# Rows of w2 in runs of four, with a different split of its last 96 rows and a different place of TensorE's loop in its code

## The chip, the cores and the metric

The kernel runs on one core of a Trainium2 chip. The metric is the device time of one execution in microseconds (us), given as the median of several runs. Profiles come from one further execution each.

## The reference

One decoding step of a transformer layer for one token of width D = 512: attention over a cache of 32 heads with 32,768 keys of width 128 each, then a dense block with a mish activation of width F = 1376. All tensors are bf16.

```python
q = layernorm(x) @ wq                                   # (512) @ (512, 32*128)
scores = einsum("bhqd,bhkd->bhqk", q, k_cache) * 128**-0.5
o = einsum("bhqk,bhkd->bhqd", softmax(scores), v_cache)
h = x + o.reshape(1, 1, 4096) @ wo                      # (4096, 512)

t = layernorm(h) @ w1 + b1                              # (512, 1376)
act = t * tanh(softplus(t))
out = h + act @ w2                                      # (1376, 512)
```

The two caches are 32 x 8 MB each. With wq and wo (4 MB each) and w1 and w2 (1.4 MB each) the kernel reads 548 MB.

## The kernel before

**Data.** `ring` holds six slots of 32 KB per partition. Keys of a head take two slots, alternating between two homes; values take the next two. A head's 32,768 rows lie so that partition p holds the 256 rows from 256p on, 64 KB in one run. At the end, the slots of the keys are used again: one for wo, one (`WL`) for wo's last 128 rows, w1 (`w1_v`) and w2 (`w2_v`).

**The queue.** SP issues all loads, in the order of the list `order`: wq, k0, then k(h+1) and v(h) in turn, wo, the last v, `WL`, four quarters of w1, the parts of w2. A load waits until TensorE has finished with what its slot held (`freed_by`, `done_with`). The first and last heads' loads are cut into pieces with semaphores of their own.

**The loop.** TensorE and VectorE run the heads in a loop. In `_pe_rounds` TensorE's code is laid out as blocks `top`, `head`, `skip`, `mid`, `tail`, `turn`, `rest`, `over`. `head` transposes the 256 key tiles of a head (L685; VectorE copies them back, L691) and multiplies them by the query (L661). `rest` finishes the softmax of the head before and multiplies its 256 value tiles by the probabilities (L712). `turn` runs once, after the first `head`; `mid` and `tail` run after the last one. `t.addr_align(256, offset=100, max_nops=0)` puts the beginning of `top` at slot 100 of a block of 256 instructions.

**The dense block.** A unit of the hidden layer is one of F's 1376 columns of w1 and rows of w2. In `mid`, b1 is transposed into `b1c` (L786, L789), and the output projection of 31 heads runs (L798). In `tail` follow the last head's projection, the second layernorm, and then three steps:

- the hidden layer (L834): for each quarter `kc` of w1 and each column j of `hid_ps`, one matmul with one output column. There are FJ + 1 = 11 columns, ten of 128 units and one of 96;
- mish on [128, 11] (L841 to L849), giving `actT`;
- the output layer (L854): for each column j, four matmuls, one for each 128 columns of the output. They lie in four strips of the array.

Units are given to columns in pairs: w2's rows 2p and 2p + 1 of a group of 256 lie in partition p, so that a DMA moves runs of two rows (2 KB). Its last 96 rows are one row per partition. `W2_J = [0, 4, 8, FJ]` are the columns at which the four DMAs of w2 begin; the matmuls of L854 wait for each DMA's semaphore at its first column. The same pairs are read from w1 by a step of two elements (`w1_pairs`).

Of the kernel before, what the change touches and what calls it, by code (L numbers as in the profile page):

```python
# [6 lines left out]
BF16 = mybir.dt.bfloat16  # L7
F32 = mybir.dt.float32
I32 = mybir.dt.int32
# [13 lines left out]
class _Sched:  # L23
# [146 lines left out]
    def _pe_rounds(self, end, head, turn, rest, mid, tail):  # L170
        from concourse.ordered_engine_set import OrderedEngineSet
        nc, e, t = self.nc, LOOPED[PE], self.engines[PE]
        on = OrderedEngineSet([e])
        names = [f"rounds_{x}_{nc.next_id()}" for x in ("top", "head", "skip", "mid", "tail", "turn", "rest", "over", "done")]
        top, n_head, n_skip, n_mid, n_tail, n_turn, n_rest, n_over, done = names
        regs = nc.alloc_registers("round", engines=on)
        nc.regs_mov(regs, 0)
        t.addr_align(256, offset=100, max_nops=0)
        nc.br(top, engines=on)
        self.reg = regs[e]  # L180
        with nc.body(top, valid_engines=on):
# [126 lines left out]
def build_kernel(nc, A_x, A_k_cache, A_v_cache, A_wq, A_wo, B_w1, B_b1, B_w2, out):  # L308
# [22 lines left out]
    FJ = F // 128  # L331
    FLAST = F - FJ * 128
    W1 = KC * F
    assert HALVES == 2 and KC == 4 and H <= 32 and FLAST > 0 and FJ % 2 == 0
    assert KC * HD == SLOT and H * D == SLOT
    W2 = W1 + (FJ + 1) * D
    assert W2 + D <= SLOT
    WB = Dh // 32

# [37 lines left out]
    perm = sb([128, 128], BF16, "perm")  # L377
    oL = sb([128, 1], BF16, "oL")
    xr = sb([1, D], BF16, "xr")
    b1r = sb([FJ // 2 + 1, 256], BF16, "b1r")  # L380
# [4 lines left out]
    hsb = sb([128, 7, FJ + 1], F32, "hsb")  # L385
    b1c = sb([128, FJ + 1], F32, "b1c")
    actT = sb([128, FJ + 1], BF16, "actT")
    outr = perm

    S_ps = ps([128, 512], "sps")  # L390
# [7 lines left out]
    C_REG = hlp[:, 129:130]  # L398
    Q_REG = hlp[:, 160:160 + H]
    L_REG = hlp[:, 200:202]  # L400
    hid_ps = S_ps[:, 0:FJ + 1]
    X_REG = hlp[:, 204:204 + 2 * KC]
    B1_REG = T_f[3][:, 0:FJ + 1]
    B1_PAIRS = T_f[3][:, 0:FJ].rearrange("p (i s) -> p s i", s=2)
    y2_ps = T_f[0][:, 0:128]
    OX_PS = T_f[2][:, 0:32]

# [105 lines left out]
    w2_v = w12[:, W1:W2].rearrange("p (j n) -> p j n", j=FJ + 1)  # L513
    wol_v = w12[:, W2:W2 + D]

    def done_with(kind, h, r0, r1):
# [18 lines left out]
    def program(S):  # L535
# [13 lines left out]
        for what in order:  # L549
# [4 lines left out]
            flat = ring[:, slot, :]  # L554
            if what[0] == "wq":
                S.wait(SP, ["b1z"])
                start(b1r[0:FJ // 2, :], B_b1[0:FJ * 128].rearrange("(i p) -> i p", i=FJ // 2), s_b1)
                start(b1r[FJ // 2:FJ // 2 + 1, 0:FLAST], B_b1[FJ * 128:F].rearrange("(o p) -> o p", o=1), s_b1)
            elif what[0] == "wo":
                start(flat, A_wo.rearrange("(p j) n -> p (j n)", j=32), ready[slot])  # L560
            elif what == WL:
# [1 line left out]
            elif what[0] == "w1":  # L563
                k = what[1]
                start(w1_v[:, k, :], B_w1[k * 128:(k + 1) * 128, :], w1_sems[k])
            elif what[0] == "w2":
                n = what[1]
                if n + 1 < len(W2_J):
                    j0, j1 = W2_J[n], W2_J[n + 1]
                    start(w2_v[:, j0:j1, :].rearrange("p (i s) n -> p i (s n)", s=2),  # L570
                          B_w2[j0 * 128:j1 * 128, :].rearrange("(i p s) n -> p i (s n)", p=128, s=2), w2_sems[n])
                else:
                    start(w2_v[0:FLAST, FJ, :], B_w2[FJ * 128:F, :], w2_sems[n])
            else:
# [12 lines left out]
                for r, n in uncut(what) if kind == "v" else later_k(h):  # L587
                    S.dma(SP, lambda r=r, n=n: sp.sem_inc(cut_sems[kind][r], 16 * n))
# [192 lines left out]
                       name=("y" if c == KC - 1 else None), waits=([f"oev{H - 1}", ready_wait(WL)] if c == 0 else ()))  # L781

        def mid():
            n_b1 = FJ // 2 + 1
            for s in range(2):
                S.step(PE, lambda s=s: t_.matmul(B1_PAIRS[:, s, :], b1r[:, :].rearrange("i (q s) -> i s q", s=2)[:, s, :],  # L786
                                                 identb[0:n_b1, 0:FJ // 2], start=True, stop=True),
                       waits=([(s_b1, 32)] if s == 0 else ()))
            S.step(PE, lambda: t_.matmul(B1_REG[:, FJ:FJ + 1], b1r[:, 0:128], identb[0:n_b1, FJ // 2:n_b1], start=True, stop=True),  # L789
                   name="b1t")  # L790
# [16 lines left out]
        def tail():  # L807
# [17 lines left out]
            S.step(ACT, lambda: a.activation(lnv, nvar, ACTF.Ln, bias=epsc[:, 0:1], scale=-1.0), name="lnln1", waits=["lnvar1", "epsc"])  # L825
            S.step(ACT, lambda: a.activation(rstd, lnv, ACTF.Exp, scale=-0.5), name="lnr1", waits=["lnln1"])
            for kc in range(KC):
                for j in range(FJ + 1):
                    W = 128 if j < FJ else FLAST
                    cols = w1_pairs[:, kc, j // 2, j % 2, :] if j < FJ else w1_v[:, kc, j * 128:F]  # L830
                    last = j == FJ and kc == KC - 1
                    waits = [(w1_sems[kc], 16)] if j == 0 else []
                    waits += ["xc1", f"exp{H - 1}"] if j == 0 and kc == 0 else []
                    S.step(PE, lambda W=W, j=j, kc=kc, last=last, cols=cols: t_.matmul(  # L834
# [12 lines left out]
            S.step(DVE, lambda: v.tensor_scalar_add(den, u, 2.0), name="den", waits=["u"])  # L847
            S.step(DVE, lambda: v.reciprocal(rden, den), name="rden", waits=["den"])
            S.step(DVE, lambda: v.tensor_tensor(actT[:, :], hu, rden, ALU.mult), name="act", waits=["rden", "hu"])  # L849
            for j in range(FJ + 1):  # L850
                W = 128 if j < FJ else FLAST
                for c in range(KC):
                    last = j == FJ and c == KC - 1
                    S.step(PE, lambda W=W, j=j, c=c: t_.matmul(  # L854
                        y2_ps[32 * c:32 * c + 1, :], actT[0:W, j:j + 1], w2_v[0:W, j, c * 128:(c + 1) * 128],
                        start=False, stop=(j == FJ), skip_group_check=True),
                        name=("y2" if last else None),
                        waits=((["act"] if j == 0 else []) + [(w2_sems[W2_J.index(j)], 16)] if c == 0 and j in W2_J else ()))
            S.step(DVE, lambda: v.tensor_copy(outr[:, :], y2_ps), name="fin", waits=["y2"])  # L859
# [49 lines left out]
```

## Time and profile before

| | |
|---|---|
| median of 3 runs | 1275.71 us (1275.57 to 1275.84) |
| the profiled execution, as timed | 1275.48 us |
| its span in the profile | 1273.6 us |
| TensorE busy, matmuls | 1016.5 us (80%) |
| VectorE busy | 715.8 us (56%) |
| bytes moved | 548.35 MB, mean 431 GB/s |
| granted TensorE clock, mean | 0.77 |

The profile counts time from the first instruction. TensorE's matmuls (PE) and weight loads (PEld) stand apart. A row of a timeline begins with start and duration; "x16" counts the instructions that it merges, and the brackets tell the idle time ahead of it and what ended it. SPq is SP's issuing of DMAs. In the chain of waits, "issue" is time in which an engine waited for nothing that the profile shows.

### The profile page before, as it was taken

The numbers are of one execution on the slowest core, as the hardware profiler recorded it, in microseconds if no ns is written. First come the engines' busy times: TensorE is split into PE (matmuls) and PEld (weight loads), VectorE is DVE, ScalarE is ACT, GpSimd is POOL, SyncE is SP. The second block draws the span as 40 slices with busy tenths as digits, with TensorE's granted clock in tenths as the row PEclk, the third lists the DMA queues.
The fourth block names the chain that finished last, engine by engine and source line by source line (L and its number), as shares of the span: only waits on it lengthen the run. The fifth ranks groups of instructions, "written<-read, shape, count | busy, mean of one in ns | idle before, by whom it ended". The sixth has DMA issues, their size and how long they took to land.

```text
span 1273.6 us, 54445 instructions
## 1 busy us (share of the span) xinstructions
PE 1016.5 (80%) x25046; PEld 988.9 (78%) x25046; DVE 715.8 (56%) x1252; ACT 20.6 (2%) x71; POOL 0.9 (0%) x8
## 2 busy tenths in 40 slices
PE   4689877779777789777788777797777897777995
PEld 4689877779777789777788777797777887777994
DVE  2566664456654466644466644566544666445661
ACT  0000000000000000000000000000000000000000
POOL 0000000000000000000000000000000000000000
PEclk9888876778877688867788776787777887677885
DMA  9999999999999999999999999999999999999998
GB/s 403 445 417 437 432 438 434 440 428 428 432 438 430 445 428 428 430 440 428 445 430 428 430 438 430 440 434 428 428 438 432 434 440 428 428 436 434 426 435 353
DMA packets 12350, 548.35 MB, mean 431 GB/s; under 512 B 1360, under 2 KB 1590, under 8 KB 2998
## 3 DMA queue, kind: packets, MB, share of 16 engines
q1 hardware_dynamic: 12340, 548.22, 99.7%
q8 instruction: 8, 0.13, 0.0%
q10 hardware_dynamic: 2, 0.00, 0.0%
HBM read 548.21 MB, written 0.00 MB: 430 GB/s over the span
## 4 chain that ended last, share of the span: by engine, by line
DMA 54%; DVE 23%; PE 18%; issue 2%; SPq 2%; POOL 0%; POOLq 0%
DMA ring<-in_A_k_cache_dram 51%; DVE ering L691 23%; PE ops L712 9%; PE tps L685 6%; DMA ring<-in_A_v_cache_dram 2%; SPq L545 2%; PE sps L661 1%; DMA ring<-in_B_w_dram 1%; PE hlp L736 1%; PE hlp L731 1%; PE hlp L746 0%; PE tps L854 0%; DVE pmax L725 0%; DVE perm L859 0%; DVE gmax L733 0%
## 5 line engine op out<-in xcount | busy, mean ns | idle before, releaser
L685 PE MATMUL tps<-identb,ring 128*128 128x128 bf16 x8192 | 668.3, 232 | 209.4 <-DMA ring<-in_A_k_cache_dram 204.9
L691 DVE COPY ering<-tps 128x1024 bf16<-128x1024 bf16 x1024 | 669.4, 692 | 259.7 <-PE tps L685 258.5
L685 PEld LDWEIGHTS tps<-identb,ring 128*128 x8192 | 522.2, 104 | 212.2 <-issue 212.2
L661 PE MATMUL sps<-qcur,ering 128*128 128x1 bf16 x8192 | 343.7, 164 | 7.7 <-DVE ering L691 6.7
L661 PEld LDWEIGHTS sps<-qcur,ering 128*128 128x128 bf16 x8192 | 309.2, 97 | 10.7 <-DVE ering L691 9.4
L712 PEld LDWEIGHTS ops<-pbuf,ring 128*128 128x128 bf16 x8192 | 226.3, 103 | 24.4 <-issue 15.1
L712 PE MATMUL ops<-pbuf,ring 128*128 128x1 bf16 x8192 | 231.3, 165 | 10.8 <-DMA ring<-in_A_v_cache_dram 8.3
L720 DVE TENSOR_TENSOR oT<-ops,rtotc 128x1 f32 x31 | 5.0, 162 | 109.8 <-PE ops L712 109.8
L733 DVE TENSOR_REDUCE gmax<-hlp 1x1 f32<-1x128 f32 x32 | 8.9, 278 | 67.5 <-PE hlp L731 67.5
L738 DVE TENSOR_SCALAR nbias<-hlp 128x1 f32<-128x1 f32 x32 | 5.1, 158 | 63.4 <-PE hlp L736 63.4
L741 ACT ACTIVATE pbuf<-sps,nbias 128x256 bf16<-128x256 f32 x32 | 15.2, 474 | 1219.9 <-PE ops L712 1166.7
L731 PE MATMUL hlp<-ident,pmax 128*1 128x128 f32 x64 | 17.9, 379 | 5.2 <-issue 5.2
L725 DVE TENSOR_REDUCE pmax<-sps 128x1 f32<-128x256 f32 x32 | 13.6, 425 | 14.3 <-PE sps L661 14.3
L736 PE MATMUL hlp<-gmax,onesmat 1*128 1x1 f32 x64 | 18.5, 356 | 0.4 <-DVE gmax L733 0.4
L736 PEld LDWEIGHTS hlp<-gmax,onesmat 1*128 1x128 f32 x64 | 15.8, 304 | 1.3 <-DVE gmax L733 0.9
L746 PE MATMUL hlp<-esum,onesmat 128*128 128x1 f32 x64 | 12.1, 258 | 4.8 <-issue 1.0
L746 PEld LDWEIGHTS hlp<-esum,onesmat 128*128 128x128 f32 x64 | 9.5, 188 | 7.4 <-issue 7.4
L640 PE MATMUL hlp<-xnT,ring 128*128 128x1 bf16 x128 | 3.6, 165 | 9.2 <-DMA ring<-in_A_wq_dram 9.2
L640 PEld LDWEIGHTS hlp<-xnT,ring 128*128 128x128 bf16 x128 | 3.5, 104 | 9.3 <-issue 9.3
L720 DVE TENSOR_TENSOR oL<-ops,rtotc 128x1 bf16<-128x1 f32 x1 | 0.2, 161 | 14.3 <-PE ops L712 14.3
L731 PEld LDWEIGHTS hlp<-ident,pmax 128*1 128x1 f32 x64 | 2.8, 81 | 5.8 <-issue 5.3
L748 DVE RECIPROCAL rtotc<-hlp 128x1 f32<-128x1 f32 x32 | 5.4, 168 | 2.7 <-PE hlp L746 1.4
(77 smaller groups left out, 40.1 us busy)
## 6 DMA issues: line engine op xcount, KB each, us to landing
ring<-in_A_k_cache_dram SPq DMA_DIRECT2D x3, 4096.0 KB, 40.2
ring<-in_A_v_cache_dram SPq DMA_DIRECT2D x3, 4096.0 KB, 15.3
ring<-in_A_k_cache_dram SPq DMA_DIRECT2D x3, 2048.0 KB, 30.5
ring<-in_A_k_cache_dram SPq DMA_DIRECT2D x1, 6144.0 KB, 44.6
ring<-in_A_wq_dram SPq DMA_DIRECT2D x1, 4096.0 KB, 12.2
ring<-in_A_wo_dram SPq DMA_DIRECT2D x1, 4096.0 KB, 35.6
ring<-in_A_v_cache_dram SPq DMA_DIRECT2D x1, 2048.0 KB, 16.1
ring<-in_B_w_dram SPq DMA_DIRECT2D x4, 344.0 KB, 20.7
```

Source lines behind the costliest of these rows:

```text
L545: S.dma(SP, lambda: sp.dma_start(dst, src).then_inc(s, 16))
L640: S.step(PE, lambda h=h, kc=kc: t_.matmul(Q_REG[:, h:h + 1], wq_v[:, kc, h * Dh:(h + 1) * Dh], xnT[:, 0, kc:kc + 1], start=(kc == 0), stop ...
L661: S.step(PE, lambda r=r: t_.matmul(S_ps[:, col0 + r:col0 + r + 1], ering[:, bg % NE, r, :], qcur[:, :], start=True, stop=True), name=(name ...
L685: S.step(PE, lambda r=r, at=at: t_.matmul(tb[:, r * 128:(r + 1) * 128], key_tile(S, at), identb[:, :], is_transpose=True, start=True, stop ...
L691: S.step(DVE, lambda: v.tensor_copy(ering[:, bg % NE, :, :].rearrange("p r d -> p (r d)"), tb[:, :]), name=f"ev{bg}", waits=[f"trb{bg}"], ...
L712: S.step(PE, lambda r=r: t_.matmul(o_ps[:, 0:1], vt[:, r, :], pbuf[:, r:r + 1], start=(r == 0), stop=(r == SCOLS - 1)), name=(names or Non ...
L725: S.step(DVE, lambda: v.tensor_reduce(pmax[:, :], S_ps[:, 0:SCOLS], AXX, ALU.max), name=f"pmax{h}", waits=[f"qkh{h}"], kind="pmax")
L731: S.step(PE, lambda: t_.matmul(A_REG, pmax[:, :], ident[:, :], start=True, stop=True), name=f"A{h}", waits=[f"pmax{h}", "ident", f"rcp{h - ...
L733: S.step(DVE, lambda: v.tensor_reduce(gmax[:, :], A_REG, AXX, ALU.max), name=f"gmax{h}", waits=[f"A{h}"], kind="gmax")
L736: S.step(PE, lambda: t_.matmul(B_REG, onesm[0:1, :], gmax[:, :], start=True, stop=True), name=f"B{h}", waits=[f"gmax{h}", "consts0"] + ([] ...
L741: S.step(ACT, lambda: a.activation(pbuf[:, :], S_ps[:, 0:SCOLS], ACTF.Exp, bias=nb[:, :], scale=SC, accum_out=esum[:, :]), name=f"exp{h}", ...
L746: S.step(PE, lambda: t_.matmul(C_REG, onesm[:, :], esum[:, :], start=True, stop=True), name=f"C{h}", waits=[f"exp{h}"], kind="C")
```

## The change

Units are given to columns in fours instead of pairs. Rows 0 to 1023 of w2 go in two DMAs of 128 partitions by four rows (4 KB runs) to columns 0 to 3 and 4 to 7, rows 1024 to 1279 as before in pairs to columns 8 and 9. [...] So there are five DMAs of w2 instead of four, and FC = 15 columns instead of 11 in the hidden layer, in mish and in the output layer. w1 is read by the steps that belong to this (`units_of`), and b1 is loaded as three rows of 512 and transposed in 11 matmuls instead of 3. `identi` now shares the memory of `ering`. The loop of TensorE begins at slot 30 of a block instead of slot 100.

```diff
-        t.addr_align(256, offset=100, max_nops=0)
+        t.addr_align(256, offset=30, max_nops=0)
...
+    FC = FJ + 5
+    W2 = W1 + FC * D
...
-    identi = sb([128, 128], I32, "identi")
+    identi = ering[:, 1, 0:2, :].rearrange("p r d -> p (r d)").bitcast(I32)
...
-    W2_J = [0, 4, 8, FJ]
+    W2_G = [(0, 0, 4, 128), (4, 512, 4, 128), (8, 1024, 2, 128), (10, 1280, 4, 20), (14, 1360, 1, F - 1360)]
+    W2_J = [g[0] for g in W2_G]
+    W2_M = [next(m for j0, _, n, m in W2_G if j0 <= j < j0 + n) for j in range(FC)]
...
-    w1_pairs = w1_v[:, :, 0:FJ * 128].rearrange("p k (i q s) -> p k i s q", q=128, s=2)
+    def units_of(rows, j):
+        j0, u0, n, m = next(g for g in W2_G if g[0] <= j < g[0] + g[2])
+        return rows[:, u0:u0 + n * m].rearrange("p (q s) -> p s q", s=n)[:, j - j0, :]
...
             elif what[0] == "w2":
                 n = what[1]
-                if n + 1 < len(W2_J):
-                    j0, j1 = W2_J[n], W2_J[n + 1]
-                    start(w2_v[:, j0:j1, :].rearrange("p (i s) n -> p i (s n)", s=2),
-                          B_w2[j0 * 128:j1 * 128, :].rearrange("(i p s) n -> p i (s n)", p=128, s=2), w2_sems[n])
-                else:
-                    start(w2_v[0:FLAST, FJ, :], B_w2[FJ * 128:F, :], w2_sems[n])
+                j0, u0, c, m = W2_G[n]
+                src = B_w2[u0:u0 + c * m, :].rearrange("(p s) n -> p (s n)", s=c)
+                if m == 20:
+                    src = src.rearrange("(a p) n -> a p n", a=5)
+                start(w2_v[0:m, j0:j0 + c, :].rearrange("p s n -> p (s n)"), src, w2_sems[n])
...
             for kc in range(KC):
-                for j in range(FJ + 1):
-                    W = 128 if j < FJ else FLAST
-                    cols = w1_pairs[:, kc, j // 2, j % 2, :] if j < FJ else w1_v[:, kc, j * 128:F]
+                for j in range(FC):
+                    W = W2_M[j]
+                    cols = units_of(w1_v[:, kc, :], j)
...
-            for j in range(FJ + 1):
-                W = 128 if j < FJ else FLAST
+            for j in range(FC):
+                W = W2_M[j]
                 for c in range(KC):
```

More of the change, by code (lines that the diff above doesn't have):

```diff
@@ L333, in build_kernel @@
     W1 = KC * F
-    assert HALVES == 2 and KC == 4 and H <= 32 and FLAST > 0 and FJ % 2 == 0
+    assert HALVES == 2 and KC == 4 and H <= 32 and FLAST > 0 and FJ == 10
     assert KC * HD == SLOT and H * D == SLOT
-    W2 = W1 + (FJ + 1) * D
+    FC = FJ + 5
+    W2 = W1 + FC * D
     assert W2 + D <= SLOT
@@ L384, in build_kernel @@
     xnT = sb([128, 2, KC], BF16, "xnT")
-    hsb = sb([128, 7, FJ + 1], F32, "hsb")
-    b1c = sb([128, FJ + 1], F32, "b1c")
-    actT = sb([128, FJ + 1], BF16, "actT")
+    hsb = sb([128, 7, FC], F32, "hsb")
+    b1c = sb([128, FC], F32, "b1c")
+    actT = sb([128, FC], BF16, "actT")
     outr = perm
@@ L400, in build_kernel @@
     L_REG = hlp[:, 200:202]
-    hid_ps = S_ps[:, 0:FJ + 1]
+    hid_ps = S_ps[:, 0:FC]
     X_REG = hlp[:, 204:204 + 2 * KC]
-    B1_REG = T_f[3][:, 0:FJ + 1]
-    B1_PAIRS = T_f[3][:, 0:FJ].rearrange("p (i s) -> p s i", s=2)
+    B1_REG = T_f[3][:, 0:FC]
     y2_ps = T_f[0][:, 0:128]
@@ L511, in build_kernel, with __getitem__ @@
     w1_v = w12[:, 0:W1].rearrange("p (k n) -> p k n", k=KC)
-    w1_pairs = w1_v[:, :, 0:FJ * 128].rearrange("p k (i q s) -> p k i s q", q=128, s=2)
-    w2_v = w12[:, W1:W2].rearrange("p (j n) -> p j n", j=FJ + 1)
+    class b1_last:
+        def __getitem__(self, at):
+            return b1r[:, at[1].start - 1024:at[1].stop - 1024]
+    def units_of(rows, j):
+        j0, u0, n, m = next(g for g in W2_G if g[0] <= j < g[0] + g[2])
+        return rows[:, u0:u0 + n * m].rearrange("p (q s) -> p s q", s=n)[:, j - j0, :]
+    w2_v = w12[:, W1:W2].rearrange("p (j n) -> p j n", j=FC)
     wol_v = w12[:, W2:W2 + D]
@@ L556, in program @@
                 S.wait(SP, ["b1z"])
-                start(b1r[0:FJ // 2, :], B_b1[0:FJ * 128].rearrange("(i p) -> i p", i=FJ // 2), s_b1)
-                start(b1r[FJ // 2:FJ // 2 + 1, 0:FLAST], B_b1[FJ * 128:F].rearrange("(o p) -> o p", o=1), s_b1)
+                start(b1r[0:2, :], B_b1[0:1024].rearrange("(i p) -> i p", i=2), s_b1)
+                start(b1r[2:3, 0:F - 1024], B_b1[1024:F].rearrange("(o p) -> o p", o=1), s_b1)
             elif what[0] == "wo":
@@ L783, in mid @@
         def mid():
[L784 to L790, printed above, removed]
+            for n in range(4):
+                S.step(PE, lambda n=n: t_.matmul(B1_REG[:, 0:8].rearrange("p (i s) -> p s i", s=4)[:, n, :],
+                                                 b1r[:, :].rearrange("i (q s) -> i s q", s=4)[:, n, :],
+                                                 identb[0:3, 0:2], start=True, stop=True),
+                       waits=([(s_b1, 32)] if n == 0 else ()))
+            for j in range(8, FC):
+                S.step(PE, lambda j=j: t_.matmul(B1_REG[0:W2_M[j], j:j + 1], units_of(b1_last(), j), identb[0:3, 2:3], start=True, stop=True),
+                       name=("b1t" if j == FC - 1 else None))
             S.step(ACT, lambda: a.copy(b1c[:, :], B1_REG), name="b1c", waits=["b1t"])
@@ L827, in tail @@
             for kc in range(KC):
-                for j in range(FJ + 1):
-                    W = 128 if j < FJ else FLAST
-                    cols = w1_pairs[:, kc, j // 2, j % 2, :] if j < FJ else w1_v[:, kc, j * 128:F]
-                    last = j == FJ and kc == KC - 1
+                for j in range(FC):
+                    W = W2_M[j]
+                    cols = units_of(w1_v[:, kc, :], j)
+                    last = j == FC - 1 and kc == KC - 1
                     waits = [(w1_sems[kc], 16)] if j == 0 else []
@@ L849, in tail @@
             S.step(DVE, lambda: v.tensor_tensor(actT[:, :], hu, rden, ALU.mult), name="act", waits=["rden", "hu"])
-            for j in range(FJ + 1):
-                W = 128 if j < FJ else FLAST
+            for j in range(FC):
+                W = W2_M[j]
                 for c in range(KC):
-                    last = j == FJ and c == KC - 1
+                    last = j == FC - 1 and c == KC - 1
                     S.step(PE, lambda W=W, j=j, c=c: t_.matmul(
                         y2_ps[32 * c:32 * c + 1, :], actT[0:W, j:j + 1], w2_v[0:W, j, c * 128:(c + 1) * 128],
-                        start=False, stop=(j == FJ), skip_group_check=True),
+                        start=False, stop=(j == FC - 1), skip_group_check=True),
                         name=("y2" if last else None),
```

3 lines of the change are left out of this document (2 added, 1 removed).

## The prediction

> **What bounds the kernel now.** I read the page first, then the chain of waits, then stretches of the end.
>
> ```profile
> span 1273.6 us, 54445 instructions
> ...
> DMA  9999999999999999999999999999999999999998
> GB/s 403 445 417 437 432 438 434 440 428 428 432 438 430 445 428 428 430 440 428 445 430 428 430 438 430 440 434 428 428 438 432 434 440 428 428 436 434 426 435 353
> ...
> q1 hardware_dynamic: 12340, 548.22, 99.7%
> q8 instruction: 8, 0.13, 0.0%
> ```
>
> The DMA engines are full in every slice but the last, and one queue's packets take 99.7% of sixteen engines' span. The other row to keep is the eight instruction packets: nearly all code is fetched once, not once per head. The middle is flat:
>
> ```profile
> 150.00:1200.00 1050.00, 846.82 (x21028) 827.88 (x21025) 602.68 (x1035) 15.26 (x54) 0.00 (x0) 0.77 1.00 434
> ```
>
> In these columns (busy of PE, PEld, DVE, ACT, POOL, then clock, DMA share, GB/s) TensorE works 847 of 1050 us. It has slack, the DMA engines have none. So the time is 548.22 MB at 434 GB/s, 1263 us, plus what happens before the queue fills, where it might run dry, and after the last data. The change leaves the bytes alone. It can act at two places only: the end, and the first two heads, where code is fetched.
>
> The end, by the chain (start, us, what):
>
> ```profile
> 1252.38 2.71 SPq L545
> 1255.13 4.57 SPq L545
> 1259.74 10.85 DMA ring<-in_B_w_dram
> 1270.63 0.54 PE tps L854 x11
> 1271.20 0.29 DVE perm L859
> ```
>
> The last link is the third part of w2 (columns j=8 and 9), issued at 1259.74 and landed at 1270.59. TensorE then needs 0.54 us, DVE 0.29, and the output's DMA the rest. The windows show how the queue ends:
>
> ```profile
> 1268.25:1268.75 0.50, 0.12 (x1) 0.00 (x0) 0.22 (x2) 0.21 (x1) 0.00 (x0) 0.50 0.89 283
> 1268.75:1270.00 1.25, 0.60 (x20) 0.33 (x22) 0.53 (x3) 0.00 (x0) 0.20 (x1) 0.50 0.46 166
> 1270.00:1270.50 0.50, 0.50 (x16) 0.29 (x16) 0.00 (x0) 0.00 (x0) 0.00 (x0) 0.50 0.17 57
> ```
>
> From 1268.75 to 1270.00 the share is 0.46: some seven of sixteen engines still move data and nine have finished. The work is spread evenly over the engines, so about seven of them run 1.3 to 1.8 us late. Seven or eight instruction packets and seven late engines suggest that each fetch holds up one engine for good; that is an inference.
>
> **The change at the end, part by part.** TensorE's and the weight loads' rows (start, us, group):
>
> ```profile
> 1253.45 3.57 PE L712 MATMUL ops<-pbuf,ring 128*128 128x1 bf16 x128 [3.96 <-DMA ring<-in_A_v_cache_dram]
> 1262.10 0.59 PE L712 MATMUL ops<-pbuf,ring 128*128 128x1 bf16 x16 [0.27 <-DMA ring<-in_A_v_cache_dram]
> 1263.41 0.59 PE L712 MATMUL ops<-pbuf,ring 128*128 128x1 bf16 x16 [0.71 <-DMA ring<-in_A_v_cache_dram]
> 1265.87 1.18 PE L834 MATMUL sps<-xnT,ring 128*128 128x1 bf16 x33 [0.30 <-issue]
> 1267.23 0.51 PE L834 MATMUL sps<-xnT,ring 128*128 128x1 bf16 x11 [0.19 <-DMA ring<-in_B_w_dram]
> 1269.40 0.28 PE L854 MATMUL tps<-ring,actT 128*1 128x128 bf16 x4 [1.02 <-DVE actT L849]
> 1269.40 0.38 PE L854 MATMUL tps<-ring,actT 128*1 128x128 bf16 x8 [1.02 <-DVE actT L849]
> 1269.40 0.49 PE L854 MATMUL tps<-ring,actT 128*1 128x128 bf16 x12 [1.02 <-DVE actT L849]
> 1269.98 0.30 PEld L854 LDWEIGHTS tps<-ring,actT 128*1 128x1 bf16 x16 [0.28 <-DMA ring<-in_B_w_dram]
> L712 PE MATMUL ops<-pbuf,ring 128*128 128x1 bf16 x8192 | 231.3, 165 | 10.8 <-DMA ring<-in_A_v_cache_dram 8.3
> ```
>
> *Hidden layer (L834).* 15 columns instead of 11, so 60 matmuls instead of 44. A matmul with one output column starts every (3.57 - 0.165) / 127 = 0.027 us. The first three quarters become 45: 1265.87 + 45 x 0.027 = 1267.08, still ahead of the last quarter of w1, which arrives at 1267.23. They stay covered, with 0.15 us to spare. In the last quarter 4 more are on the path: 4 x 0.027 = +0.11. The columns are now read at a step of four elements instead of two. The nearest row is the transposition of x at the start, half of whose reads step by four:
>
> ```profile
> 2.23 0.40 PE L613 MATMUL hlp<-identb,xr 1*128 1x1 bf16 x8 [2.23 <-DVE identb L609]
> ```
>
> With 164 ns for one, (0.40 - 0.16) / 7 = 0.034 us each. At that price the 45 end at 1267.40, 0.17 past the landing, and the last 15 take another 0.10: upper bound +0.38. Lower bound +0.05, if narrow tiles of 20 and 16 columns are cheaper than the 96 of before. I take +0.11, since the stepped reads of L834 already keep 0.027 to 0.032 apart (1.18 us for 33).
>
> *mish (L841 to L849).* 15 columns instead of 11.
>
> ```profile
> L843 DVE TENSOR_SCALAR hsb<-hsb 128x11 f32<-128x11 f32 x1 | 0.2, 174 | 0.0
> ```
>
> The cast of 128 columns in the chain above takes 0.29 and this one of 11 takes 0.17, so four columns add 0.004 each, 0.03 over seven operations.
>
> *w2's DMAs.* The two large parts change from 2 KB to 4 KB runs. Of before, the issue rows say:
>
> ```profile
> ring<-in_B_w_dram SPq DMA_DIRECT2D x2, 512.0 KB, 15.5
> ```
>
> The second part lands at about 1269.94 (TensorE goes on at 1269.98), 14.8 after its issue at 1255.13. So the first took 16.2 from 1252.38 and landed at 1268.6: 512 KB in 2 KB runs take about 1.37 us. V's last two pieces are 512 KB in 4 KB runs, and TensorE resumes on them at 1262.10 and 1263.41: 1.31. Two parts give -0.12. Bounds: nothing (the third part, 256 KB in 2 KB runs, needs 0.65 from 1269.94 to 1270.59, as fast as the 4 KB runs), and -0.4 if 4 KB went at the full 434 GB/s (1.21 us, 0.16 less a part, and a little for fewer packets). I take -0.15: the third part lands at 1270.48.
>
> The last 96 rows were six 1 KB rows on each engine, behind the third part. [...] One more issue on SP is hidden: it issued the third part 10.85 us ahead of its landing.
>
> [...]
>
> *Output layer (L854).* Four matmuls, one column j, take 0.28; eight 0.38, twelve 0.49: 0.105 for each further j. Before, three j's followed the landing at 1270.59; now seven follow (8 and 9, 10 to 13, 14). TensorE gets there in time: it starts at 1269.40 + 0.11 + 0.03 = 1269.54, and eight j's end by 1269.54 + 0.28 + 7 x 0.105 = 1270.56, of which the last 0.28 is pipeline. From the landing: 1270.48 + 0.04 + 0.28 + 6 x 0.105 = 1271.43, against 1270.63 + 0.54 = 1271.17. So **+0.26**, of which the four j's are +0.42 and the earlier landing -0.15. Cast, output and epilogue are as before. Bounds: 0.0 (the landing 0.4 earlier) and +0.5 (stepped loads make TensorE late).
>
> **The loop's place in memory.** The loop's start moves from slot 100 to slot 30 of a 256-instruction block, and the code grows by 40 matmuls (8 for b1, 16, 16) with their weight loads: 80 instructions. On the first pass the chain shows holes that no data explains:
>
> ```profile
> 39.29 1.06 issue
> 45.44 2.13 issue
> 51.54 4.71 issue
> 87.37 2.50 issue
> 40.30:45.50 5.20, 5.08 (x121) 4.91 (x121) 4.39 (x7) 0.00 (x0) 0.00 (x0) 1.00 1.02 438
> 86.48 7.01 SPq L545 DMA_DIRECT2D ring<-in_A_v_cache_dram  x2
> ```
>
> Between the first two holes lie 121 matmuls with 121 loads, which with the loop's register writes is one block of 256: TensorE waits for the next block. The page's eight instruction packets leave none for the later passes, so the loop stays resident. All later blocks of the head begin 70 instructions later, 70/256 x 5.1 = 1.4 us. [...] Hence pass two, and the first half of v1, which waits for TensorE at 86.48, come at 87.9.
>
> Is the queue dry by then? Ahead of it are wq and k0, k1, v0, k2: 37.75 MB. A slice is 31.84 us; two give 12.8 and 14.2 MB, the rest at 417 GB/s ends at 89.5, later on the late engines. A first transfer shows the latency:
>
> ```profile
> 0.74 0.39 SPq L869 DMA_DIRECT2D ring<-in_A_wq_dram  x1
> 0.00:1.00 1.00, 0.00 (x0) 0.00 (x0) 0.10 (x3) 0.00 (x0) 0.38 (x5) 1.00 0.00 0
> 1.00:2.00 1.00, 0.00 (x0) 0.00 (x0) 0.91 (x6) 0.72 (x1) 0.36 (x3) 1.00 1.37 361
> ```
>
> Data flows at most 1.26 us after the issue: 87.9 + 1.26 = 89.2, still 0.3 ahead. So the shift costs nothing, with little cover: whatever TensorE loses beyond that on an engine is lost at the end. Below nothing it can't go, as the queue is full already.
>
> [...]
>
> **Sum.** +0.26 at the end, 0 in front. The profiled execution took 1275.48 (span 1273.6 and 1.9 around it), 0.23 below the median of 1275.71: 1275.74 for that execution, 1275.97 for the median, say **1275.9**, since the largest doubts at the end (faster landing) point down. A kernel like this can be told from no change at about 0.2%, 2.55 us, so this is no change.
>
> **Rivals.**
> 1. [...] Chance 0.22.
> 2. *The landing gains more.* -0.4 there, and the seven j's are paid in part while waiting: -0.1 to -0.3, 1275.5. Against it the 0.65 of the third part. Chance 0.13.
> 3. *Slower: the queue runs dry before v1.* If the moved blocks cost a further hole like that of 51.54 (4.71), v1 comes at 92.6; data at 93.9, 4.4 us after the queue's end, and nothing later gives it back: 1280. It decides from 1.7 us of delay on, of which 1.4 are used. Small overruns (to 1 us) hit engines that aren't late and are free. Chance 0.06.
> 4. *Slower: the loop stays no longer resident.*
>
> ```profile
> L685 PE MATMUL tps<-identb,ring 128*128 128x128 bf16 x8192 | 668.3, 232 | 209.4 <-DMA ring<-in_A_k_cache_dram 204.9
> L661 PE MATMUL sps<-qcur,ering 128*128 128x1 bf16 x8192 | 343.7, 164 | 7.7 <-DVE ering L691 6.7
> ```
>
> With L712's 8192 these give the loop's end: 774 matmuls with loads per head (8192/32 x 3 + 6) are 1548 instructions, by the listing some 80 register, wait and branch instructions, 90 and 196 for `mid` and `tail`, 12 for the rest: about 1927. Slot 100 + 1927 = 2027 lies in the eighth block; 30 + 1927 + 80 = 2037 does too, 11 short of its end at 2048. If I miscounted by more, a ninth block is needed on each of 31 passes: nine waits of some 7 us (39.29 + 1.06 to 45.44 + 2.13 is 7.2) make 65 us a pass instead of 39: about 2080. Chance 0.02. [...]
>
> **How the numbers follow.** Forecast 0.57, its own range 1275.6 to 1276.2. The range reaches over rivals 1 and 2, 1275.3 to 1276.8, and leaves out 3 and 4 and the edges. Slower by over 0.2% are rivals 3 and 4, 0.07, as a hundredth of 3 comes out below 2.55 us. Within 0.2% are the forecast, 1 and 2 and that hundredth, 0.93, less 0.02 for faster by over 0.2%: with a share of 1.00 in the middle and 1.8 us between the first engine's end and the last's, I see no place for more.
>
> **What would show it.** Right: the holes 70 instructions later, none after 95 us; v1 issued near 88; the share 1.00 in the middle; L834 x15 near 0.6; L854 with seven j's behind the last wait. [...]

## The result

The change makes the kernel slower: 1278.63 us (median of 14 runs, 1276.93 to 1279.32) against 1275.53 (14 runs, 1275.24 to 1275.88). The ratio is 1.0022, 95% interval 1.0015 to 1.003. The forecast of 1275.9 and its range of 1275.3 to 1276.8 missed it. The spread is new as well: before varies by 0.6 us, after by 2.4. Of one kernel further on, a single execution at a granted clock of 0.61 instead of 0.77 took 1314.63 us and is left out of its figures.

The profiled execution of after took 1278.77 us, 3.3 more than that of before. Its page:

```profile
span 1276.9 us, 54526 instructions
...
DMA  9999999999999999999999999999999999999998
...
DMA packets 12039, 548.37 MB, mean 429 GB/s; under 512 B 1366, under 2 KB 1514, under 8 KB 2686
...
q1 hardware_dynamic: 12028, 548.22, 99.5%
q8 instruction: 9, 0.15, 0.0%
```

Bytes are the same, and there is one instruction packet more. The middle is unchanged (share 1.00 and 433 GB/s from 150 to 1200 us). The end, in the rows that answer to those of before:

```profile
1265.37 0.59 PE L726 MATMUL ops<-pbuf,ring 128*128 128x1 bf16 x16 [0.71 <-DMA ring<-in_A_v_cache_dram]
1267.83 2.53 PE L851 MATMUL sps<-xnT,ring 128*128 128x1 bf16 x60 [0.30 <-issue]
1272.06 1.86 PE L871 MATMUL tps<-ring,actT 128*1 128x128 bf16 x60 [0.98 <-DVE actT L866]
1273.98 0.29 DVE L876 CAST perm<-tps 128x128 bf16<-128x128 f32 x1 [1.97 <-PE tps L871]
1274.30 0.60 SPq L603 DMA_DIRECT2D out_dram<-perm  x1
```

Before, V's last piece was read at 1263.41, the hidden layer ran from 1265.87 to 1267.74, the output layer began at 1269.40, the cast at 1271.20, and the output's issue was this row of before:

```profile
1271.52 0.61 SPq L589 DMA_DIRECT2D out_dram<-perm  x1
```

The differences make the budget:

| step | before | after | more |
|---|---|---|---|
| V's last piece read, hidden layer begins | 1263.41, 1265.87 | 1265.37, 1267.83 | 1.96, from the front |
| hidden layer | 1.87 | 2.53 | 0.66 |
| its end to the cast | 3.46 | 3.62 | 0.16 |
| output's issue to the end of the span | 2.1 | 2.6 | 0.5 |

So w2's runs aren't the matter at all: in after nothing waits for w2 any more (the output layer waits only for `actT`), and the largest item comes in before 1263 us. The chain of waits of the first two heads (start, us, what) and SP's issues (a row's first number is the issue of the first DMA) show where:

```profile
17.86 5.50 issue
34.59 0.75 issue
40.39 2.21 issue
49.08 1.05 issue
52.81 5.83 issue
89.11 3.19 issue
```

```profile
23.35 3.59 PE L699 MATMUL tps<-identb,ring 128*128 128x128 bf16 x32 [6.71 <-issue]
88.36 7.69 SPq L560 DMA_DIRECT2D ring<-in_A_v_cache_dram  x2
128.52 0.33 SPq L560 DMA_DIRECT2D ring<-in_A_v_cache_dram  x1
```

The same two rows of before:

```profile
18.24 3.59 PE L685 MATMUL tps<-identb,ring 128*128 128x128 bf16 x32 [1.61 <-DMA ring<-in_A_k_cache_dram]
125.39 0.33 SPq L545 DMA_DIRECT2D ring<-in_A_v_cache_dram  x1
```

There is a new hole of 5.50 us at the entry of the loop, the hole at `turn` is 5.83 instead of 4.71, the one at 89 is 3.19 instead of 2.50. v1 was issued 1.88 later than before (86.48), v2 3.13 later. The queue ends 1.96 later.

### The profile page after: what moved, and what is told of

Same layout as the page of the kernel before. It is cut to its first block, busy times and chain, and to the rows that moved or that the text cites. A ratio compares the mean times of both kernels' runs of the same rounds, so it can differ in the third digit from the quotient of the medians.

```text
span 1276.9 us, 54526 instructions
## 1 busy us (share of the span) xinstructions
PE 1016.4 (80%) x25086; PEld 989.3 (77%) x25086; DVE 715.7 (56%) x1252; ACT 20.8 (2%) x71; POOL 1.2 (0%) x8
## 2 busy tenths in 40 slices
DMA packets 12039, 548.37 MB, mean 429 GB/s; under 512 B 1366, under 2 KB 1514, under 8 KB 2686
## 4 chain that ended last, share of the span: by engine, by line
DMA 54%; DVE 23%; PE 20%; issue 3%; SPq 1%; POOL 0%; ACT 0%; POOLq 0%
DMA ring<-in_A_k_cache_dram 50%; DVE ering L705 23%; PE ops L726 9%; PE tps L699 7%; DMA ring<-in_A_v_cache_dram 4%; PE sps L675 1%; PE hlp L750 1%; PE hlp L745 1%; SPq L560 0%; PE hlp L760 0%; PE sps L851 0%; PE tps L871 0%; PE hlp L836 0%; POOL b1r L614 0%; DVE pmax L739 0%
```

## The experiments

Each kernel is set beside runs of before from the same group; before's medians there were 1275.46, 1275.52 and 1275.47 (27 to 33 runs each). A ratio with its interval in brackets is not the quotient of the medians. The theory (A in the first expectations) was: the code's new place delays TensorE in the first heads, v1 and v2 come too late, and the queue loses about 2 us. Rival B put the whole difference on the dense block at the end.

**The place alone.** Before, with one number changed.

```diff
-        t.addr_align(256, offset=100, max_nops=0)
+        t.addr_align(256, offset=30, max_nops=0)
```

> The kernel before with the loop at slot 30 and nothing else changed. Theory A (code): the loop's place alone makes TensorE late in the first two heads, v1 and v2 come too late to SP's queue and the DMA engines stand idle for a while: v1 issued near 88, nine instruction packets, end 1.9 us later, 1277.4. Theory B (data): the loss comes from the new runs of w2 and the longer dense block: no change, 1275.5.

Measured: 1277.03 (1275.35 to 1277.57), ratio 1.0009 [1.0000, 1.0018]. In its trace, with the dense block of before:

```profile
q8 instruction: 9, 0.15, 0.0%
...
88.12 7.15 SPq L545 DMA_DIRECT2D ring<-in_A_v_cache_dram  x2
127.82 0.33 SPq L545 DMA_DIRECT2D ring<-in_A_v_cache_dram  x1
1266.93 1.18 PE L834 MATMUL sps<-xnT,ring 128*128 128x1 bf16 x33 [0.30 <-issue]
```

v1 and v2 are late, there is a ninth packet, and the hidden layer begins 1.06 later. About 1.5 us in the median come from the place alone, half of the change. The interval just touches no change (three of the eleven runs are as fast as before's), so it is the trace with which B falls as the whole cause.

**After, at slot 38.**

```diff
-        t.addr_align(256, offset=30, max_nops=0)
+        t.addr_align(256, offset=38, max_nops=0)
```

> The changed kernel with the loop at slot 38 instead of 30. If slot 30 is before the end of the code that precedes the loop, the loop begins one block later and needs one fetch more; slot 38 is behind that end. Theory A: one instruction packet fewer, the hole of 5.5 us at 17.86 gone, v1 issued near 87.6 instead of 88.4, half of the loss of 2.0 in front gone: 1277.6. Theory B: 1278.6.

Measured: 1277.65 (1276.76 to 1279.41), ratio 1.0020 [1.0011, 1.0029]. The number fits, its reason doesn't: the profile still has nine packets, and the first key matmul comes at 22.14 after a hole of 5.46. So the code ahead of the loop ends beyond slot 38 as well (and before slot 100, where before has no such hole); the ninth packet fits a first block of the loop that has to be fetched in both. What helps is that in the profiled execution (1277.06) TensorE had caught up by v1:

```profile
86.40 7.41 SPq L560 DMA_DIRECT2D ring<-in_A_v_cache_dram  x2
1265.90 2.53 PE L851 MATMUL sps<-xnT,ring 128*128 128x1 bf16 x60 [0.30 <-issue]
1272.36 0.60 SPq L603 DMA_DIRECT2D out_dram<-perm  x1
```

With v1 on time the hidden layer begins as in before (0.03 later). That execution lost 1.6 us all the same, all of it behind 1265.9: the end's part, seen by itself. Nine packets, as in after, so the further packet alone doesn't make the queue late.

**The turn's code next to the head's.** If the jump to `turn` is what is dear, put its block directly behind `head`, so that it is reached without a far jump.

```diff
+        with nc.body(n_turn, valid_engines=on):
+            turn()
+            nc.regs_alu(regs, regs, 1, op=ALU.add)
+            nc.br(top, engines=on)
...
-        with nc.body(n_turn, valid_engines=on):
-            turn()
-            nc.regs_alu(regs, regs, 1, op=ALU.add)
-            nc.br(top, engines=on)
```

> The changed kernel with the code of turn placed directly behind that of head, so that the jump to it stays in a block that TensorE already has. Theory A: the hole of 5.83 us at 52.81 goes, v1 is issued before 85 and v2 before 126, the queue does not run dry and the end comes 2.0 us earlier: 1276.7. Theory B: TensorE's time in front does not matter, 1278.6.

Measured: 1278.82 (1276.83 to 1280.18), 1.0023 [1.0013, 1.0032]. A miss, and the chain says why:

```profile
48.84 2.34 issue
...
80.04 4.98 issue
...
88.89 7.29 SPq L563 DMA_DIRECT2D ring<-in_A_v_cache_dram  x2
1268.84 2.53 PE L854 MATMUL sps<-xnT,ring 128*128 128x1 bf16 x60 [0.30 <-issue]
```

The hole at `turn` is gone; one of 4.98 has come up at 80.04, 13 matmuls into the first pass of `rest`. In after that code lies directly behind `turn`'s, and there is no hole there. With nine packets in both, the fetch had not been removed but put off, nearer to v1: 88.89, and the hidden layer 2.97 late.

**The hidden layer with plain columns.** All 60 matmuls read 128 adjacent columns of w1 (others than the reference's).

```diff
-                    W = W2_M[j]
-                    cols = units_of(w1_v[:, kc, :], j)
+                    W = 128
+                    cols = w1_v[:, kc, 88 * j:88 * j + 128]
```

> The changed kernel with the 60 matmuls of the hidden layer reading plain columns of 128 units at a step of one instead of steps of four and tiles of 20 and 16 (so the hidden layer is computed from other columns of w1). Theory A for the end: stepped reads at 0.033 each and the change between wide and narrow tiles, 0.1 each time, cost 0.75 of the 2.5 us; the group takes about 1.75 and the end comes 0.75 earlier: 1277.9. Rival: the hidden layer waits for w1 and w2 anyway and the end does not move by more than 0.1: 1278.5.

Measured: 1278.9 (1276.51 to 1280.06), 1.0023 [1.0014, 1.0032]. The front varies by more than the effect, so the time decides nothing. The profiled execution (1276.56) had v1 at 86.16, and there the rows do:

```profile
1265.89 1.92 PE L851 MATMUL sps<-xnT,ring 128*128 128x1 bf16 x60 [0.30 <-issue]
1270.58 0.10 PEld L871 LDWEIGHTS tps<-ring,actT 128*1 128x1 bf16 x8 [0.32 <-DMA ring<-in_B_w_dram]
1270.90 0.41 PEld L871 LDWEIGHTS tps<-ring,actT 20*1 20x1 bf16 x20 [0.21 <-DMA ring<-in_B_w_dram]
```

1.92 instead of 2.53 for the same count: the form of the reads, steps and narrow tiles together, costs 0.61. And with TensorE early enough to wait for w2, one sees the third part's landing: 1270.58, 0.05 earlier than in before. The 0.21 ahead of the first load of 20 partitions, put down to w2, is no such sign, for the same gap stands in after, where that part had landed 0.57 earlier (1272.66):

```profile
1273.23 0.41 PEld L871 LDWEIGHTS tps<-ring,actT 20*1 20x1 bf16 x20 [0.22 <-issue]
```

**The extra block alone.** Before at slot 100, with 36 of the query projection's matmuls made twice (72 instructions), which brings the end of the code ahead of the loop past slot 100 and leaves the borders within the loop in place.

```diff
-            for kc in range(KC):
+            for kc in list(range(KC)) * (2 if h < 9 else 1):
```

> The kernel before, loop at slot 100 as it was, with 36 matmuls of the first nine heads' query projection done twice ahead of the loop (72 instructions more), so that the loop's block is one further on and isn't there when the code ahead of it ends. Theory A (one block more to fetch, at the jump to the loop): the jump takes 4 to 5 us, the first key matmul comes at 22 instead of 18.2, one instruction packet more, v1 near 88; 1277.0, some runs as before. Theory C (what counts is where the block borders cut the head): the borders are where they were, 1275.5.

Measured: median 1276.84, ratio 1.0006 [0.9997, 1.0015]. The runs lie between 1275.24, as in before, and 1277.71. The interval takes in no change, so this speaks for a cost by itself (+1.3 in the median) without proving it; the trace is of the execution that was left out, and isn't used.

**The borders alone.** After, with 36 of the query projection's matmuls left out (for heads 0 to 17 half of the sum is missing; the loop is the same), so that the code ahead ends before slot 30.

```diff
-            for kc in range(KC):
+            for kc in range(2 if h < 18 else KC):
```

> The changed kernel with 36 matmuls of the query projection left out ahead of the loop (half of the sum for heads 0 to 17), 72 instructions, so that slot 30 lies in a block that is there when the loop begins. Theory A: no long jump, first key matmul at 18.2, one instruction packet fewer, v1 near 87, no loss in front; the end's 1.3 stay: 1276.8. Theory C: the borders are where the change put them, 1278.6.

Measured: 1278.59 (1277.13 to 1280.02), 1.0022 [1.0013, 1.0031]: no faster than after. Eight packets again, and the first hole is gone, yet v1 is late:

```profile
18.39 3.39 PE L699 MATMUL tps<-identb,ring 128*128 128x128 bf16 x32 [2.56 <-DMA ring<-in_A_k_cache_dram]
29.20 1.03 PE L699 MATMUL tps<-identb,ring 128*128 128x128 bf16 x8 [4.66 <-DMA ring<-in_A_k_cache_dram]
...
41.32 2.69 issue
50.44 0.76 issue
53.88 4.72 issue
89.55 3.02 issue
88.79 7.53 SPq L560 DMA_DIRECT2D ring<-in_A_v_cache_dram  x2
```

TensorE stands 4.66 us for k0's second piece until 29.20, and the holes lie 2.0 to 2.4 later than those of before at 39.29 and 51.54. The moved borders suffice without the extra block.

**Taking the deadline away.** After, with v1 and v2 cut into 64, 64 and 128 rows instead of 128 and 128 (v1) or one piece (v2), so that each first piece is issued sooner. The last head's V takes its cuts from the same list, so its first 128 rows come in two pieces as well.

```diff
-    V_EVENTS = (TPS,)
+    V_EVENTS = (TPS // 2, TPS)
...
-    CUTS = {"k": [64, 192], "v": [TPS, 192, 224, 240]}
+    CUTS = {"k": [64, 192], "v": [TPS // 2, TPS, 192, 224, 240]}
...
-            at = [TPS] if what in (("k", 1), ("v", 1)) else ...
+            at = [TPS // 2, TPS] if what in (("v", 1), ("v", 2)) else [TPS] if what == ("k", 1) else ...
```

> The changed kernel with the values of heads 1 and 2 loaded in three pieces (64, 64 and 128 rows of each partition) instead of two and one, each as soon as TensorE has done with what lies there, 2 to 5 us earlier; TensorE's own delay stays. Theory A (the delay costs time by a dry queue alone): TensorE is as late as before, but the first piece of v1 is issued near 86 and of v2 near 124, nothing is lost in front: 1276.8. Rival: the loss has another way than SP's queue: 1278.6.

Measured: 1277.25 (1276.93 to 1277.75), 1.0011 [1.0002, 1.0020].

```profile
17.90 5.51 issue
...
52.80 5.59 issue
...
86.23 10.11 SPq L560 DMA_DIRECT2D ring<-in_A_v_cache_dram  x3
122.78 6.42 SPq L560 DMA_DIRECT2D ring<-in_A_v_cache_dram  x3
1266.24 2.54 PE L851 MATMUL sps<-xnT,ring 128*128 128x1 bf16 x60 [0.30 <-issue]
```

TensorE's holes are as long as in after, but the hidden layer begins 0.37 late instead of 1.96, and the spread falls from 2.4 to 0.8 us. TensorE's delay as such cost nothing here; what cost was the queue that waited for it. This settles the front, down to the 0.37, which is no more than the finer pieces cost in before (0.45, below).

**The last instructions.** The same, with the loop at slot 20, where it ends at slot 2027 as in before; its first block is still an extra one (a hole of 4.38 at 18.02, nine packets).

```diff
-        t.addr_align(256, offset=30, max_nops=0)
+        t.addr_align(256, offset=20, max_nops=0)
```

> As a_early, and the loop at slot 20 instead of 30, so that the last instructions of TensorE lie in a block that is there. Theory: the 0.5 us between the output's landing and the end of the span go as well; what is left is the longer dense block, +0.7 on the kernel before: 1276.2. Rival: the end of TensorE's code does not set the end of the span: as a_early.

Measured: 1276.56 (1276.41 to 1278.48, nine of eleven below 1276.8), 1.0008 [0.9999, 1.0017], 0.7 below the kernel before this one. The profiled execution is the slowest, 1278.48: there v1 was issued at 89.01 in spite of the finer pieces, and the hidden layer began 2.19 late. The end of its span:

```profile
span 1276.6 us, 54532 instructions
...
1274.53 0.60 SPq L603 DMA_DIRECT2D out_dram<-perm  x1
```

2.1 from the output's issue to the end, as in before, against 2.6 in after, and 2.8 in the kernel at slot 38. Over the profiles: 2.0 to 2.1 where the loop's code ends by slot 2027, 2.6 to 3.1 where it ends at 2037 to 2045. What SP waits for at the very end, first in after, then in before:

```profile
SPq L887 <- PEq L887: 0.7, 1, 0.7
SPq L870 <- PEq L870: 0.2, 1, 0.2
```

SP waits for TensorE, whose last jump, from 1273.27 on, lasts 3.28 us in after, with an instruction packet at 1274.23, and 0.31 in before. All kernels of the second group have such a long jump (3.3 to 3.8 us) and a further instruction packet behind the end of the span (in after at 1277.31), so not in the page's count; none of the first group has either. By the jump and the packets, TensorE's last instructions there lie in a block that must still be fetched. In the last kernel below, whose loop reaches into that block itself, the end takes 2.0 again.

**Fewer changes of width.** The same, with the hidden layer's wide tiles (128 units) and narrow ones (20 and 16) in groups: two changes instead of seven.

```diff
-            for kc in range(KC):
-                for j in range(FC):
+            turns = [(kc, js) for js in (wide, narrow) for kc in range(KC - 1)] + [(KC - 1, narrow), (KC - 1, wide)]
+            for kc, js in turns:
+                for j in js:
```

> As a_fix (values of heads 1 and 2 in three pieces, loop at slot 20), with the hidden layer's 60 matmuls in another order: the ten wide columns of the first three quarters of w1, then their narrow columns of 20 and 16 units, then the last quarter's narrow ones, then its wide ones. Theory (each change between wide and narrow tiles costs 0.1): two or three changes instead of eight, the group takes 2.0 instead of 2.53 and the end comes 0.5 earlier than with a_fix: 1276.05. Rival (the reads at a step of four are the cost, the changes are not): 2.5 again, 1276.55.

Measured: 1276.12 (1275.96 to 1276.35), 1.0004 [0.9995, 1.0013].

```profile
1266.25 2.09 PE L854 MATMUL sps<-xnT,ring 128*128 128x1 bf16 x60 [0.30 <-issue]
```

2.09 instead of 2.53 to 2.54: 0.45 for five changes, 0.09 each.

**Five engines in fact.** In the trace of after, the part of 80 rows (columns 10 to 13, in fours to 20 partitions) lands in ten shares, at 1270.98 to 1272.66, where w2's other parts land in sixteen: by that count it was spread over ten engines, not over the five that the outermost dimension of its source (`a=5`) was meant for. The packets under 512 B fit: the early pieces add 64 with four more DMAs, 16 each, and the change adds 6 (1360 to 1366), which are 10 for these rows, less 3 for the completions of b1's fewer rows and less one short row of b1. So this one, otherwise as the kernel at slot 20, starts them as four DMAs of five partitions (10 more small packets, 1440 against 1430: 20 instead of 10, five for each DMA).

```diff
-                start(w2_v[0:m, j0:j0 + c, :].rearrange("p s n -> p (s n)"), src, w2_sems[n])
+                for p in range(0, m, 5 if m == 20 else m):
+                    q = p + (5 if m == 20 else m)
+                    start(w2_v[p:q, j0:j0 + c, :].rearrange("p s n -> p (s n)"), src[p:q, :], w2_sems[n])
```

> As a_fix, with the 80 rows of w2 in four DMAs of five partitions each, which use five engines, where the changed kernel's one DMA of 20 partitions ran on ten. Theory (TensorE is behind the data by then): no change, 1276.55. Rival (the last rows' placing on the engines sets the end): up to 0.6 earlier or later.

Measured: 1276.51 (1276.36 to 1277.52), 1.0008 [0.9999, 1.0017], as without it. How the 80 rows are spread did not set the end (1276.51 against 1276.56).

**Before with the early pieces.** The three edits of the early pieces, in before.

> The kernel before with the values of heads 1 and 2 in three pieces each, issued earlier. Theory: the queue did not run dry in most runs of before, so the median stays, 1275.5; its few runs of 1277 to 1278.4, which come when v1 is issued late, are gone. Rival (the finer pieces cost issue time or short packets): 1275.8 or more.

Measured: 1275.81 (1275.64 to 1275.92), 1.0002 [0.9992, 1.0011]. The rare late runs of before (four of 33 above 1276.9 in the group of the early pieces, one of 27 in this) don't come up in these eleven, at 0.3 us in all the others; the hidden layer begins at 1266.32, 0.45 later. It is no faster. No version beat before.

**The loop out of its room.** After at slot 100, where the loop's code ends at slot 2107; timed once.

> The changed kernel with the loop at slot 100 as before, so that its code (2007 instructions by my count) ends at slot 2107, beyond eight blocks of 256. Theory: the loop no longer stays resident, some code is fetched again on each of 31 passes, dozens to hundreds of instruction packets instead of nine or ten, TensorE's passes take longer than the 39 us of a head's data and the time rises by hundreds of us, up to 2080. Rival (eight blocks are no limit): ten packets, 1276 to 1279.

Measured: 1669.14 us. Its page:

```profile
DMA  9996778877779676897777967779777788767876
...
q8 instruction: 281, 4.60, 1.1%
...
PE 63%; issue 31%; DVE 3%; DMA 3%; SPq 0%; POOL 0%; ACT 0%; POOLq 0%
```

281 packets are nine for nearly every pass: by that count, with 70 slots more all of the loop's code is fetched anew on each pass.

## Why the prediction was wrong

**The failed step** is "the shift costs nothing". It took the latency of the first transfer, 1.26 us, as the lead that v1's issue needs, found 0.3 us of cover before the queue's end at 89.5, and called overruns of up to 1 us free. The queue ended later than that and lost all the same. The trace has the times at which a load's sixteen shares landed, as many as there are DMA engines; here each share is taken for one engine's. Those of k2, the load ahead of v1, landed from 90.15 to 92.06 (before: 90.06 to 92.08), so the issue at 88.36 led the first engine's end by 1.8 us; for v2 (128.52) the lead was 1.2. In before the leads were 3.6 at both and nothing was lost, nor with 3.8 and 3.3 at slot 38. The four kernels with leads of 1.2 to 2.0 (before at slot 30, after, the turn's code next to the head's, the borders alone) lost 1.06 to 2.97. From k2's first share to that of v1's first half they took 0.7 to 1.0 us longer than the kernels with enough lead (10.5 to 10.7 against 9.7 to 9.8); with their leads that makes an estimate of 2.1 to 2.8 us from an issue to its data on a full queue, where the prediction had 1.26.

That engines which aren't late lose up to 1 us for free was in part right: in v1's first half seven shares were late already, and they landed as in before (101.6 to 101.9, before 101.4 to 101.8). But two others came behind them all, at 102.34 and 103.00. By the last share the queue fell 1.2 us behind before's at v1's first half, 0.6 more at v2, and 0.1 after: the 1.96 of the budget, and none of it came back. Why those two lost more than the rest isn't shown, since the trace doesn't say which engine a share belongs to.

**The delay itself** was forecast at 1.4 and was 1.88 at v1, because the hole at `turn` grew with it, and 3.13 at v2, which the prediction never looked at: the hole at 89.11 grew too, and it stands between v1 and v2. The long hole came at 52.81, 1.27 later than in before, near the 1.4.

**The block ahead.** The prediction moved the loop's start by 70 slots without asking where the code ahead of it ends. It ends between slots 38 and 100 of its block (there is a first hole with slot 38 and none with slot 100 in before), so the start moved into a new block, and the jump met code that wasn't there: 5.50 us at 17.86, and nine packets instead of eight. Without that hole TensorE waits for k0 instead (4.66 us until 29.20, in the borders experiment), so it isn't what made v1 late by itself.

**Rival 3** (the queue runs dry before v1) is what happened, with 2.0 us for the front instead of 4.4, and without the further long hole that it had been made to need. Its chance of 0.06 rested on that need and on "from 1.7 us of delay on". A share below 0.9 near 90 us or over nine packets is no mark for it: nine packets came, and the share from 90 to 92 us was 0.83 in after and 0.69 in before, where nothing was lost.

**The hidden layer** was the term mis-sized: +0.11 forecast with a bound of +0.38, +0.66 measured. Plain reads took 1.92, and 1265.87 + 1.92 = 1267.79 would have been +0.05 on 1267.74: the count of matmuls was priced rightly. The rest, 0.61, is the seven changes between wide and narrow tiles, 7 x 0.09 = 0.63 by the grouped kernel, and 32 loads at a step of four, which keep 0.033 apart instead of 0.027 (0.19), less the 0.18 for which the kernel with plain columns still waits for the last quarter of w1. The lower bound, "if narrow tiles of 20 and 16 columns are cheaper", saw half: the narrow loads do come 0.025 apart, and changing to them and back costs more than they save.

**mish and the output layer**: 1.66 to 1.70 from the hidden layer's end to the first output matmul, +0.04 (forecast +0.03); and 1.80 to 1.92 to the cast. The forecast of +0.42 for the four j's and -0.15 for the landing met neither condition, since TensorE is too late to wait: it reaches columns 8, 10 and 14 at 1272.77, 1273.23 and 1273.51, and their last shares had landed at 1272.42, 1272.66 and 1272.83. In the kernel with plain columns, where it arrives in time, the third part gained 0.05 and not 0.15. No trace shows the change's 80 rows on five engines, where the forecast and rival 1 had them: they landed in ten shares, in the kernel with plain columns the last three at 1270.55 to 1270.81 and the others by 1269.64. So late ones are among them, but a price doesn't show. The load of j = 10 comes 0.32 behind that of j = 9 in that kernel and 0.36 behind it in after, where nothing is waited for, so the change to 20 partitions covers the late shares.

**The epilogue** was "as before", and cost 0.5: the program's last instructions lie behind the loop's code, and the count of 2037 slots, right for the loop, left them out. The jump to them takes 3.28 us instead of 0.31.

**Right** were the middle, the mechanism of the place (later blocks, later v1), and the count of the loop's code: with its end at slot 2037 (2045 in the kernel at slot 38) nine packets bring the code for all passes, with its end at 2107 there are 281. The prediction had no row for a bound of eight blocks; by its count of slots the runs put the bound between 2045 and 2107. Rival 4's price was not right: 12.7 us a pass ((1669.14 - 1275.47) / 31) instead of 26. A pass there takes 51.7 us (from 592.53 to 644.23), of which the holes are 16.8; the rest is 34.9 and not 39, an estimate of 4 us a pass that had been waits for data.

Its inference that each fetch of code holds up one DMA engine for good fits as well. In before the number of shares that land over 1 us behind the first is none at 17 us, 2 at 27 to 29, 3 at 42 to 44, 4 at 51 to 53, 6 at 71 to 73 and 7 at 90 to 92, each time as many as the instruction packets up to then (18.54, 27.14, 38.00, 45.21, 53.64, 60.63, 87.37), and it stays 7. In after, with eight packets by 90, it is 8. They come 1.4 to 2.1 us behind. One packet more did not move the last share: at slot 38, with eight as well, that of v1's first half landed at 101.86, in before at 101.79.

**Open** is why the holes on the first pass vary from run to run. Kernels with the extra block and the moved borders had v1 at 86.2 to 86.4 in two profiles and at 88.4 to 88.9 in two others, though one of the first has after's code up to there, and the spread of after's times is most likely this. Nor can the borders' and the block's shares in after's 1.96 be told apart: the borders are enough, the block by itself is likely but not shown to be. The grouped kernel's 0.3 over before with the early pieces (1276.12 against 1275.81) is, by the two traces, 0.16 in the hidden layer (2.09 against 1.93) and 0.22 from the first output matmul to the cast (1.97 against 1.75), which with small differences elsewhere come to the 0.3; that the 0.22 is the 16 more matmuls is plausible and wasn't tried.

## What to carry over

Where one queue is full all the time, look for the deadline of each issue that waits for a computing engine, and measure its lead: from the issue to the moment when the first DMA engine runs out. Here leads of 3.3 us and more lost nothing, those of 2.0 and less did, and none between was measured. TensorE's delay was free only up to there, and of the 1.96 us that the queue of after lost nothing came back by the end. Moving the loop by 70 slots put v1's issue 1.64 us later in before (86.48 to 88.12), and in after the last jump took 3.28 us instead of 0.31: work out where the code ahead of a loop ends, where the loop ends, and where the program's last instructions lie. Count the changes of tile shape (here seven, at 0.09 us each), not only the matmuls.

## What was unexpected in the hardware

- A border between blocks cost much on the first pass of after, with a full DMA queue: from hole to hole 7.3 us (34.59 + 0.75 = 35.34 to 40.39 + 2.21 = 42.60) against 5.1 of running time. A jump to code that wasn't there took 4.1 to 5.8 us (4.07 at 51.93 in before with the early pieces, 5.83 at 52.81 in after), also for the first entry of the loop (5.50 at 17.86 in after).
- Between end slots 2037 and 2107 the time went from 1278.63 to 1669.14 us and the instruction packets from nine to 281. With the end at 2037 nine packets were enough for 32 passes of eight blocks.
- Changing between 128-wide and 16- or 20-wide stationary tiles (those of the PEld rows) cost about 0.09 us each time (0.45 for five changes). A load at a step of four bf16 elements came 0.033 us behind the one before (L851 of after), at a step of two (L834 of before) or one (L712 of before) 0.027.
- A DMA written as five by four with a destination of 20 partitions landed in ten shares (1270.98 to 1272.66 in after).
- In before the number of shares that landed over 1 us behind the first rose with the instruction packets, from none at 17 us to 7 at 90, each 1.4 to 2.1 us behind, and was 7 still in V's last piece (1261.41 to 1263.36). That each packet held up one DMA engine is inferred from this.
- Cutting three loads (v1, v2 and the last V) into finer pieces took the median of before from 1275.47 to 1275.81 us, and the hidden layer began 0.45 later.
